# Three weight transfers at the seam change their order, and four sums move into the next step

## The chip, the cores and the metric

One core of a Trainium2 chip runs the whole kernel. The metric is the device time of one execution in microseconds. TensorE is called PE (its weight loads PEld), VectorE DVE, ScalarE ACT, GpSimd POOL; SP is the engine that issues most transfers.

## The reference

Two blocks follow one another. The first is a Mamba-2 scan over 4 batches, 8 heads, 768 positions in chunks of 32. The second routes 3072 tokens of 256 channels to one of 8 experts by a hash of the token's id:

```python
for c in range(nc):
    M = einsum('bhin,bhjn->bhij', Cc, Bc) * (exp(cum_i - cum_j) * causal)
    y[:, :, sl] = einsum('bhij,bhjd->bhid', M, xc) + einsum('bhin,bhnd->bhid', Cc, state) * exp(cum)
    state = decay_full * state + sum(Bx)
x = y.transpose(0, 2, 1, 3).reshape(3072, 256)
expert_idx = token_ids * 2654435761 % 8
for e in range(8):                     # w1[e]: 256 x 1024, w2[e]: 1024 x 256
    mask = expert_idx == e
    out[mask] = maximum(x[mask] @ w1[e], 0) @ w2[e]
```

## The kernel before, in words

The order on every engine is written out by hand; each engine and each DMA queue takes its instructions in that order, and waits by semaphores.

**First part.** The scan goes over 12 pieces of 64 positions in each sequence, two for each turn of a loop over `k`. Beside it the routing is worked out. Experts are sorted by their token count; what comes out first is *place* 0, the next place 1, and so on. The tokens of place `p` go into slots of a long row, in two halves (`p`, 0) and (`p`, 1) of `HALF[p]` tokens (202, 200, 198, 192, ...). The row is cut into tiles of 128 tokens. The first halves of places 0 to 3 lie in tiles 0 to 6, whose tokens are known early; tiles 7 and 8 hold the second half of place 0.

**Second part.** Each expert's two matrix products are done by a scheme with seven products instead of eight: `up(p, q0, what)` is one of the seven of the first layer for two of its four column blocks, `down(p, what)` one of the second layer's. Products 1 and 2 of `up` read only the first halves of the weights (`k` = 0, 1 of columns 0 to 511) and of the tokens. The others read sums: `sums_x` over tokens (DVE), `sums_w(p, layer, i, engine)` over weights (128 x 512 elements each, both operands in SBUF, four for a place and layer), `sums_h` over the hidden rows (DVE). Each `up` group is four matmuls into a PSUM bank of its own, and DVE or ACT drains the bank before the next product on it.

**The weights.** `load_w1(p, i)` asks for half `i` of place `p`'s first matrix (512 KB) on SP's queue; `load_w2(p)` for the second matrix (1 MB). (0, 0), (0, 1), (1, 0) and (2, 0) are asked for inside the first part. Place 3's buffer lies in memory that the first part gives back.

**The seam.** Between the parts stands the stretch from line 1025 to 1053. SP asks for (1, 1), (2, 1) and (3, 0), and POOL for the gathers of tiles 7, 8, 9 and 10. Then follow 16 groups (`m` = 0 to 15), products 1 and 2 of places 0 to 3, in the order of `seq`: the last four (`m` = 12 to 15) are place 3's and read (3, 0). DVE turns early tiles (`early`), and makes place 0's second two weight sums at `m` = 5, place 1's four at `m` = 8 and place 2's four at `m` = 11. At `m` = 13 and 14 PE turns tile 7 and tile 8, ahead of that `m`'s matmuls (`turn`: two transposes into bank 6, a copy by ACT); at `m` = 15 DVE makes the four sums over place 0's tokens. Behind the first group SP has a transfer of four bytes that waits for tile 8's gather (`held`), and behind that `load_w2(0)`, `load_w1(3, 1)` and `load_w2(1)`.

**The steps.** `step(p)` runs rounds `r`: in each a product of `up` for place `p`, both column blocks, and one of `down` for place `p - 1`. Step 0 has five rounds (products 6, 7, 5, 4, 3) and no `down`. POOL makes the weight sums of the second layer in it, `sums_w(0, 2, i)`, one in a round. DVE drains the banks, makes the sums over place 1's tokens from round 2 on, and begins step 1 with `sums_h(0, 0)`.

Of the kernel before, what the change touches and what calls it, by code (L numbers as in the profile page):

```python
# [25 lines left out]
def kernel(  # L26
# [12 lines left out]
    dve, act, pe, pool_e, sp_e = nc.vector, nc.scalar, nc.tensor, nc.gpsimd, nc.sync  # L39
# [7 lines left out]
    E, _, F = moe_w1.shape  # L47
# [564 lines left out]
    def load_w1(p, i, eng=sp_e):  # L612
        if p not in w1s:
            w1s[p] = (w4[0] if p % 4 == 3 else wpool).tile([P, DP, F], F32, name="w1")
        src = moe_w1[bass.ds(regs[p], 1), :, i * FH:(i + 1) * FH].rearrange("e (k p) f -> p (e k) f", p=P)
        eng.dma_start(out=w1s[p][:, :, i * FH:(i + 1) * FH], in_=src)

    def load_w2(p, eng=sp_e):
        w2s[p] = wx[0].tile([P, FP, DM], F32, name="w2", bufs=2)
        eng.dma_start(out=w2s[p], in_=moe_w2[bass.ds(regs[p], 1)].rearrange("e (k p) d -> p (e k) d", p=P))  # L620
# [139 lines left out]
    def early(m):  # L760
        turn_pair([q for q in EK if q // 2 == m], (3, 2, 7, 6)[m], dve)
# [3 lines left out]
    def sums_w(p, layer, i, eng):  # L765

        if layer == 1:
            w = w1s[p]
            q = lambda i, k: w[:, k, i * FH:(i + 1) * FH]
            if p not in s1:  # L770
                s1[p] = (spool if p % 3 else s1pool).tile([P, 4, FH], F32, name="s1")
            s = s1[p]
        else:
            w = w2s[p]
            q = lambda i, k: w[:, k * Q4:(k + 1) * Q4, i * P:(i + 1) * P]
            if p not in s2:
                s2[p] = spool.tile([P, 4, Q4, P], F32, name="s2")
            s = s2[p]
        i = (2, 1, 3, 0)[i]
        a_, b_, o = ((q(1, 0), q(1, 1), OP.add), (s[:, 2], q(1, 1), OP.add), (q(1, 0), q(0, 0), OP.subtract),  # L780
                     (q(0, 1), s[:, 1], OP.subtract))[i]
        eng.tensor_tensor(out=s[:, i], in0=a_, in1=b_, op=o)  # L782
        if eng is pool_e and i in (0, 3):
            eng.tensor_copy(out=space, in_=s[:, i, 0, 0:1] if layer == 2 else s[:, i, 0:1])
# [90 lines left out]
    def sums_x(p, i):  # L875
        n = HALF[p]
        q = lambda k, j: xT[:, k, slots(p, j)]
        if i == 0:
            t1[p] = mwork.tile([P, 4, N0], F32, name="t1")
        t = t1[p][:, :, 0:n]  # L880
        a_, b_ = ((q(0, 1), q(0, 0)), (q(1, 1), t[:, 0]), (q(0, 1), q(1, 1)), (q(1, 0), t[:, 1]))[i]
        dve.tensor_tensor(out=t[:, i], in0=a_, in1=b_, op=OP.subtract)  # L882

    def sums_h(p, i):
        n = HALF[p]
        if i == 0:
            t2[p] = hpool.tile([P, 4, Q4, N0], F32, name="t2", bufs=1)
        t = t2[p][:, :, :, 0:n]
        q = lambda k, j: hx[p][:, {(0, 1): 0, (1, 0): 1, (1, 1): 2}[k, j], :, 0:n]
        if i == 0:  # L890
            dve.scalar_tensor_tensor(out=t[:, 0], in0=q(0, 1), scalar=0.0, in1=h11[p][:, :, 0:n],
                                     op0=OP.max, op1=OP.subtract)
        elif i == 1:
            dve.tensor_tensor(out=t[:, 1], in0=q(1, 1), in1=t[:, 0], op=OP.subtract)
        elif i == 2:
            dve.scalar_tensor_tensor(out=t[:, 2], in0=q(0, 1), scalar=0.0, in1=q(1, 1), op0=OP.max, op1=OP.subtract)  # L896
        else:
            dve.tensor_tensor(out=t[:, 3], in0=q(1, 0), in1=t[:, 1], op=OP.subtract)
# [100 lines left out]
    def scatter(o_sb, idx):  # L999
        st = pool_e.indirect_dma_start(  # L1000
            out=out[:], out_offset=bass.IndirectOffsetOnAxis(ap=idx, axis=0),
            in_=o_sb, in_offset=None, bounds_check=NT - 1, oob_is_err=False)
        tc.declare_no_dep(st.ins, group="out_rows", reason="distinct rows")
        tc.add_to_no_dep_group("out_rows", st.ins)
# [12 lines left out]
    def turn(k):  # L1017
        if k not in turned:
            turn_x(k, XB)
            turned.add(k)  # L1020
# [1 line left out]
    need = lambda p: [k for k in tiles_of(p) if k not in EK] if p < E else []  # L1022
    outs = sorted(range(NK), key=lambda k: (done_at[k], k))

    for w in ((1, 1), (2, 1), (3, 0)):
        load_w1(*w)
    ask(need(0))
    first = [(p, q0) for p in range(NEAR) for q0 in (0, 2)]
# [3 lines left out]
    for m, (what, i) in enumerate(seq):  # L1032
        if m in (2, 6, 10):
            early((m + 2) // 4)
        if m == 5:
            for j in range(2, 4):
                sums_w(0, 1, j, dve)
        if m == 8:
            for j in range(4):
                sums_w(1, 1, j, dve)  # L1040
        if m == 11:
            for j in range(4):
                sums_w(2, 1, j, dve)
        if m in (13, 14):
            turn(need(0)[m - 13])
        if m == 15:
            for j in range(4):
                sums_x(0, j)
        up(*first[i], what, banks=(i % 6,) * 2)
        if m == 0:  # L1050
            sp_e.dma_start(out=held[:], in_=xg[need(0)[-1]][0:1, 0:1])
            for w in (0, (3, 1), 1):
                load_w2(w) if isinstance(w, int) else load_w1(*w)

    UP = [1, 6, 2, 7, 5, 4, 3]
    UP_E = [6, 7, 5, 4, 3]
    DOWN = [1, 2, 6, 5, 7, 4, 3]

    def step(p):

        ups = [] if p == E else UP_E if p < NEAR else UP
        downs = DOWN if p > 0 else []
        turns = [k for k in need(p + 1) if k not in turned]
        puts = [k for k in outs if done_at[k] == p - 2]
        gets = [k for w in ((2,), (3, 4))[p] for k in need(w) if k not in asked] if p < 2 else need(p + 3)
        sums = [(p, 2, i) for i in range(4)] if p < E else []
        sums += [(p + 2, 1, i) for i in range(4)] if 0 < p < E - 2 else []
        xs_ = [(p + 1, i) for i in range(4)] if p + 1 < E else []
        R = 5 if p == 0 else 7
        off = 0 if p == 0 else (R - len(ups)) // 2  # L1070
        sent = []
        for r in range(R):
            if p > 0 and (r == 0 or p >= NEAR and r < 4):
                sums_h(p - 1, r)
            if sent:
                scatter(*sent.pop(0))
            if gets and p == 0:
                ask(gets)
                gets = []
            if 0 <= r - off < len(ups):  # L1080
                up(p, 0, ups[r - off])
            if turns:
                turn(turns.pop(0))
            if puts:
                sent.append(put(puts.pop(0)))
            if sums and not (p == 1 and r < 4):
                sums_w(*sums.pop(0), pool_e)
            if gets and r >= 1:
                ask([gets.pop(0)])
            if 0 <= r - off < len(ups):  # L1090
                up(p, 2, ups[r - off])
            if 0 < p < NEAR and 0 < r < 4:
                sums_h(p - 1, r)
            if sums and r == 3 and p != 1:
                sums_w(*sums.pop(0), pool_e)
            if p >= NEAR and r >= 3 and not turns and xs_:
                sums_x(*xs_.pop(0))
            if p == 1 and r == 4:
                pool_e.tensor_copy(out=space, in_=t2[0][:, 3, 0, 0:1])
            if p == E - 1 and r == R - 1:  # L1100
                sums_h(p, 0)
            if downs:
                down(p - 1, downs[r])
                if downs[r] == 4 and p + 1 < E:
                    load_w2(p + 1)
            if p < NEAR and r >= (2 if p == 0 else 3) and not turns and xs_:
                sums_x(*xs_.pop(0))
        while xs_ or turns:
            if turns:
                turn(turns.pop(0))  # L1110
            else:
                sums_x(*xs_.pop(0))
        for o in sent:
            scatter(*o)
        for v in sums:
            sums_w(*v, pool_e)
        if p + 4 < E:
            load_w1(p + 4, 0)
            load_w1(p + 4, 1)
        for k in gets:  # L1120
            ask([k])

    for p in range(E):
        step(p)
# [48 lines left out]
    for m in range(2):  # L1173
        scatter(o_own[m], idx_out[:, rest[m]:rest[m] + 1])

    _, rn = nc.values_load_multi_w_load_instructions(
        nov_i[0:1, 0:1], min_val=0, max_val=NCH + E,
        skip_runtime_bounds_check_because="a count of tiles: at most one an expert besides the full ones")
    kf = route.tile([P, 1], F32)
    dve.memset(kf, float(NK))  # L1180
    with tc.For_i(0, rn[0], 1):
# [9 lines left out]
        for c in range(NCH):  # L1191
# [14 lines left out]
        _, re = nc.values_load_multi_w_load_instructions(  # L1206
            ei_i[0:1, 0:1], engines=[ET.SP], min_val=0, max_val=E - 1,
            skip_runtime_bounds_check_because="an expert's number, clamped to E - 1")
# [52 lines left out]
```

## Time and profile before

| | us |
|---|---|
| three runs | 231.1, 235.72, 237.67 |
| their median | 235.72 |
| the profiled execution | 231.41 |
| its span | 229.7 |
| PE busy | 213.5 |
| DVE busy | 180.7 |
| POOL busy | 172.4 |

The profile is that of one execution; its times count from the start of the span. The granted clock of PE was full up to the end of the work.

### The profile page before, as it was taken

The numbers are of one execution on the slowest core, as the hardware profiler recorded it, in microseconds if no ns is written. First come the engines' busy times: TensorE is split into PE (matmuls) and PEld (weight loads), VectorE is DVE, ScalarE is ACT, GpSimd is POOL, SyncE is SP. The second block draws the span as 40 slices with busy tenths as digits, with TensorE's granted clock in tenths as the row PEclk, the third lists the DMA queues.
The fourth block names the chain that finished last, engine by engine and source line by source line (L and its number), as shares of the span: only waits on it lengthen the run. The fifth ranks groups of instructions, "written<-read, shape, count | busy, mean of one in ns | idle before, by whom it ended". The sixth has DMA issues, their size and how long they took to land.

```text
span 229.7 us, 5853 instructions
## 1 busy us (share of the span) xinstructions
PE 213.5 (93%) x2266; PEld 200.5 (87%) x2266; DVE 180.7 (79%) x314; ACT 89.4 (39%) x190; POOL 172.4 (75%) x220
## 2 busy tenths in 40 slices
PE   6889989998786899999999999999999999999990
PEld 2778878877685799999999999999999999999980
DVE  7868899798547688899997998697489979956630
ACT  4774965954443551312123214234323411413210
POOL 7977367866717198489988998999799999996342
PEclk9999999999999999999999999999999999999996
DMA  6999799999888885029019119307005112401011
GB/s 136 162 200 127 181 191 177 174 185 302 273 218 259 253 267 199 24 75 332 30 62 334 64 47 339 118 7 244 26 24 204 33 45 79 175 23 47 24 70 43
DMA packets 49877, 33.16 MB, mean 144 GB/s; under 512 B 26632, under 2 KB 44184, under 8 KB 49850
## 3 DMA queue, kind: packets, MB, share of 16 engines
q1 hardware_dynamic: 46786, 25.76, 45.6%
q0 software_dynamic: 2400, 6.43, 8.5%
q10 hardware_dynamic: 664, 0.61, 1.1%
q8 instruction: 18, 0.29, 0.5%
q14 instruction: 9, 0.07, 0.1%
HBM read 26.49 MB, written 6.42 MB: 143 GB/s over the span
## 4 chain that ended last, share of the span: by engine, by line
PE 73%; DMA 8%; DVE 7%; ACT 6%; issue 2%; SPq 1%; POOL 1%; ACTq 0%; DVEq 0%; POOLq 0%
PE ps L964 31%; PE ps L917 28%; PE ps L315 4%; DMA w<-in_moe_w_dram 3%; DMA xg<-y_tokens,idx_in 3%; PE ps L991 2%; PE ps L374 2%; PE ps L636 2%; DMA y_tokens<-y_sb 2%; DVE m L321 1%; ACT z L358 1%; PE ps L387 1%; PE ps L269 1%; DVE rows L259 1%; ACT ct L289 1%
## 5 line engine op out<-in xcount | busy, mean ns | idle before, releaser
L628 POOL DMA_INDIRECT xg<-y_tokens,idx_in x25 | 30.2, 1206 | 17.1 <-issue 10.1
L917 PE MATMUL ps<-t,s 128*128 128x202 f32 (+7 forms) x192 | 37.1, 328 | 0.6 <-DVE t L882 0.6
L782 POOL TENSOR_TENSOR s<-w 128x512 f32<-128x512 f32 x26 | 33.2, 1277 | 5.7 <-DMA w<-in_moe_w_dram 5.5
L1000 POOL DMA_INDIRECT out_dram<-o_sb,idx_out x25 | 26.4, 1056 | 12.5 <-ACT o_sb L996 6.7
L964 PE MATMUL ps<-t,s 128*128 128x202 f32 (+7 forms) x192 | 35.5, 326 | 0.0
L917 PEld LDWEIGHTS ps<-t,s 128*128 128x128 f32 x192 | 31.5, 190 | 1.3 <-ACT h L927 0.9
L964 PEld LDWEIGHTS ps<-t,s 128*128 128x128 f32 x192 | 31.8, 189 | 0.3 <-issue 0.3
L917 PE MATMUL ps<-xT,w 128*128 128x200 f32 (+7 forms) x128 | 24.9, 329 | 3.0 <-DMA w<-in_moe_w_dram 2.3
L917 PEld LDWEIGHTS ps<-xT,w 128*128 128x128 f32 x128 | 20.7, 190 | 3.8 <-DVE s L782 2.5
L945 ACT ACTIVATE hx<-hx 128x404 f32<-128x404 f32 (+7 forms) x16 | 8.3, 525 | 31.8 <-DVE hx L944 31.3
L321 DVE COPY_PREDICATED m<-cmask,ps 128x1024 f32<-128x1024 int32 x12 | 15.5, 1320 | 3.6 <-PE ps L315 3.6
L782 POOL TENSOR_TENSOR s<-w,s 128x512 f32<-128x512 f32 x13 | 17.6, 1351 | 0.5
L782 POOL TENSOR_TENSOR s<-s,w 128x512 f32<-128x512 f32 x13 | 17.3, 1327 | 0.5
L882 DVE TENSOR_TENSOR t<-xT 128x202 f32<-128x202 f32 (+7 forms) x16 | 16.4, 1024 | 0.8 <-ACT xT L642 0.8
L923 ACT ACTIVATE p<-ps 128x404 f32<-128x404 f32 (+7 forms) x16 | 7.9, 492 | 20.0 <-PE ps L917 19.7
L374 PEld LDWEIGHTS ps<-x_t,m 128*64 128x64 f32 x384 | 12.1, 138 | 3.0 <-issue 1.3
L374 PE MATMUL ps<-x_t,m 128*64 128x64 f32 x384 | 13.4, 224 | 1.1 <-ACT y_sb L401 0.6
L315 PE MATMUL ps<-ce,bt 32*64 32x128 f32 x384 | 12.9, 274 | 1.1 <-ACT ce L289 0.7
L882 DVE TENSOR_TENSOR t<-xT,t 128x202 f32<-128x202 f32 (+7 forms) x16 | 13.7, 854 | 0.0
L896 DVE SCALAR_TENSOR_TENSOR t<-hx 128x808 f32<-128x808 f32 (+7 forms) x8 | 13.3, 1660 | 0.0
L315 PEld LDWEIGHTS ps<-ce,bt 32*64 32x64 f32 x384 | 10.4, 132 | 2.5 <-ACT ce L289 0.9
L358 ACT ACTIVATE z<-z,half 128x256 f32<-128x256 f32 x22 | 10.0, 504 | 6.6 <-DVE z L352 6.6
(201 smaller groups left out, 472.5 us busy)
## 6 DMA issues: line engine op xcount, KB each, us to landing
w<-in_moe_w_dram SPq DMA_DIRECT2D x16, 512.0 KB, 7.1
w<-in_moe_w_dram SPq DMA_DIRECT2D x8, 1024.0 KB, 8.0
x_t<-in_x_dram SPq DMA_DIRECT2D x12, 256.0 KB, 6.2
y_tokens<-y_sb SPq DMA_DIRECT2D x10, 256.0 KB, 4.3
raw<-in_B_dram SPq DMA_DIRECT2D x12, 128.0 KB, 3.5
raw<-in_C_dram SPq DMA_DIRECT2D x12, 128.0 KB, 3.5
y_tokens<-y_sb ACTq DMA_DIRECT2D x2, 256.0 KB
xg<-y_tokens,idx_in POOLq DMA_INDIRECT x25, 3.5
```

The source lines that it names most:

```text
L315: pe.matmul(out=ps[u * T:(u + 1) * T, GB + g, b * P:(b + 1) * P].rearrange("q (e i) -> q e i", e=2), lhsT=bts[ck][r, b, c], rhs=ces[ck][r, ...
L321: dve.copy_predicated(out=m_sb[k % 2][:, g0:g1].rearrange("q g b i -> q g (b i)"), mask=cmask.bitcast(I32).rearrange("q j i -> q (j i)").u ...
L358: act.activation(z4s[un][:, :, j], zs[un].rearrange("q b e d -> q b (e d)"), AF.Copy, scale=half4[:, j:j + 1])
L374: pe.matmul(out=o, lhsT=m_sb[k % 2][:, g, b, e * T:(e + 1) * T], rhs=xs[k][:, b, 2 * g + e], start=first(g // 2 * 2 + b % 2, c), stop=True ...
L628: pool_e.indirect_dma_start(out=xg[k], out_offset=None, in_=y_dram[0:n, :], in_offset=bass.IndirectOffsetOnAxis(ap=idx_in[:, k:k + 1], axi ...
L782: eng.tensor_tensor(out=s[:, i], in0=a_, in1=b_, op=o)
L882: dve.tensor_tensor(out=t[:, i], in0=a_, in1=b_, op=OP.subtract)
L896: dve.scalar_tensor_tensor(out=t[:, 2], in0=q(0, 1), scalar=0.0, in1=q(1, 1), op0=OP.max, op1=OP.subtract)
L917: pe.matmul(out=ps[:, bank, i * n:(i + 1) * n], lhsT=lhs[:, (q0 + i) * P:(q0 + i + 1) * P], rhs=rhs, start=(first and i == 0), stop=True, ...
L945: act.activation(hq(2), hq(2), AF.Relu)
L964: pe.matmul(out=ps[:, bank, 0:n], lhsT=lhs(q), rhs=rhs(q), start=(first and q == 0), stop=True, skip_group_check=True)
L1000: st = pool_e.indirect_dma_start(out=out[:], out_offset=bass.IndirectOffsetOnAxis(ap=idx, axis=0), in_=o_sb, in_offset=None, bounds_check= ...
```

## The change

The three transfers of the seam are asked for as (1, 1), (3, 0), (2, 1). The four sums of place 2's first layer leave the seam, and DVE makes one of them behind each of the first four rounds' `up` groups in step 0.

```diff
-    for w in ((1, 1), (2, 1), (3, 0)):
+    for w in ((1, 1), (3, 0), (2, 1)):
         load_w1(*w)
...
-        if m == 11:
-            for j in range(4):
-                sums_w(2, 1, j, dve)
...
+    late_sums = [0, 1, 2, 3]
...
             if p == E - 1 and r == R - 1:
                 sums_h(p, 0)
+            if p == 0:
+                for _ in range((1, 1, 1, 1, 0)[r]):
+                    sums_w(2, 1, late_sums.pop(0), dve)
             if downs:
                 down(p - 1, downs[r])
```

## Rows read from the trace of the kernel before

**Rows 1.** The page, busy time of each engine (share of the span) and instructions.

```profile
PE 213.5 (93%) x2266; PEld 200.5 (87%) x2266; DVE 180.7 (79%) x314; ACT 89.4 (39%) x190; POOL 172.4 (75%) x220
```

**Rows 2.** Waits of PE, 56 to 125 us: who for whom, total, times, longest.

```profile
PE ps L917 <- DMA w<-in_moe_w_dram: 2.3, 1, 2.3
```

**Rows 3.** Chain that ended last, in order of time: start, us, what.

```profile
66.55 7.14 DMA w<-in_moe_w_dram
...
76.53 0.38 DVE t L882
```

**Rows 4.** Timeline of the seam: start, us, engine, line, operation, count, idle before.

```profile
69.97 0.69 DVE L782 TENSOR_TENSOR s<-w 128x512 f32<-128x512 f32 x1 [1.98 <-DMA w<-in_moe_w_dram]
70.02 1.53 PE L917 MATMUL ps<-xT,w 128*128 128x198 f32 x8
...
72.97 0.68 DVE L782 TENSOR_TENSOR s<-w 128x512 f32<-128x512 f32 x1
...
73.82 0.89 PE L917 MATMUL ps<-xT,w 128*128 128x192 f32 x4 [2.27 <-DMA w<-in_moe_w_dram]
...
74.43 0.32 SPq L1051 DMA_DIRECT2D held<-xg  x1
74.55 0.38 PE L636 MATMUL ps<-ident,xg 128*128 128x128 f32 x2
...
75.13 0.38 ACT L642 ACTIVATE xT<-ps 128x256 f32<-128x256 f32 x1
...
75.57 0.44 PE L636 MATMUL ps<-ident,xg 128*128 128x128 f32 x2
...
77.34 0.49 ACT L927 ACTIVATE h<-ps 128x384 f32<-128x384 f32 x1 [0.16 <-PE ps L917]
...
77.89 0.95 PE L917 MATMUL ps<-t,s 128*128 128x202 f32 x4 [0.58 <-DVE t L882]
```

**Rows 5.** POOL's timeline, then gathers issued from 68 to 69 us: count, us to landing.

```profile
68.26 1.00 POOL L628 DMA_INDIRECT xg<-y_tokens,idx_in  x1 [5.31 <-DMA y_tokens<-y_sb]
...
xg<-y_tokens,idx_in POOLq DMA_INDIRECT x1, 5.8
```

**Rows 6.** Timeline of step 0 and the start of step 1.

```profile
80.71 1.27 POOL L782 TENSOR_TENSOR s<-w 128x512 f32<-128x512 f32 x1 [5.46 <-DMA w<-in_moe_w_dram]
...
83.33 0.36 DVE L882 TENSOR_TENSOR t<-xT 128x200 f32<-128x200 f32 x1
...
84.70 0.36 DVE L882 TENSOR_TENSOR t<-xT,t 128x200 f32<-128x200 f32 x1
...
86.07 0.51 DVE L882 TENSOR_TENSOR t<-xT 128x200 f32<-128x200 f32 x1
...
86.77 0.99 DVE L891 SCALAR_TENSOR_TENSOR t<-hx,h 128x808 f32<-128x808 f32 x1
...
86.96 1.51 PE L917 MATMUL ps<-t,s 128*128 128x200 f32 x8
...
87.84 1.25 DVE L932 TENSOR_TENSOR u<-ps,p 128x400 f32<-128x400 f32 x2
...
89.01 1.00 DVE L894 TENSOR_TENSOR t<-hx,t 128x808 f32<-128x808 f32 x1
...
89.69 1.52 PE L917 MATMUL ps<-t,s 128*128 128x200 f32 x8
...
91.04 1.53 PE L964 MATMUL ps<-t,s 128*128 128x202 f32 x8
```

**Rows 7.** Busy time in a stretch: length, then PE, PEld, DVE, ACT, POOL.

```profile
78.95:86.77 7.82, 7.82 (x48) 7.61 (x48) 6.77 (x14) 3.31 (x7) 5.62 (x6) 1.00 0.88 281
```

**Rows 8.** Timeline of step 1's end and step 2's start.

```profile
101.07 1.90 DVE L882 TENSOR_TENSOR t<-xT 128x198 f32<-128x198 f32 x1
...
101.46 1.28 POOL L782 TENSOR_TENSOR s<-w 128x512 f32<-128x512 f32 x1
...
103.75 0.83 PE L917 MATMUL ps<-t,s 128*128 128x198 f32 x4
```

## The prediction

> **What bounds the kernel now.** I read the page first: TensorE (PE) is busy for 213.5 of 229.7 us [rows 1], so time is saved only where PE stands still, and lost where it is made to. Second, who PE waited for between 56 and 125 us: the longest wait, 2.3 us once, is for a weight transfer [rows 2]. Third, the chain of work that ended last, in order of time: a weight transfer issued at 66.55 and landing 7.14 later, at 73.69, is a link of it [rows 3]. The reader is to see that this is place 3's first half, (3,0), the last of the three transfers that the seam asks for, and that PE went idle at 70.02 + 1.53 = 71.55 and began that place's matmuls at 73.82 [rows 4]. So the order of the three transfers is on the path.
>
> Fourth, what else arrives just then. The seam's last matmul groups stand behind two turned tiles, 7 and 8. Tile 7's gather was issued at 68.26 and landed 5.8 later, at 74.06 [rows 5]. Tile 8's landing is seen on SP: the small transfer that waits for it alone started at 74.43 [rows 4]. Both come after (3,0). So PE's 2.3 us can't all be won: two more arrivals lie 0.4 and 0.7 us behind the one that is moved.
>
> Fifth, VectorE (DVE) in step 0. Between its first drain there, at 78.95, and the start of the first sum over the hidden rows, at 86.77, it was busy for 6.77 of 7.82 us [rows 6, 7]. It has 1.05 us free there, and the change puts four operations in.
>
> **The change, part by part.** *(3,0) goes second.* The transfer that is second now landed by 72.97, since DVE's sums from it started then without waiting for a transfer [rows 4]; the first landed before 69.97. Equal transfers in the same place should land alike, so (3,0) lands between 71.8 (halfway from 69.97 to 73.69) and 72.97; I take 72.4, an estimate. PE starts the first group 0.13 after the landing now (73.69 to 73.82), so at 72.5; its four matmuls are done by 73.4. Then it meets tile 7: landed 74.06, with the same 0.13 the turn starts at 74.2 instead of 74.55. ScalarE's (ACT's) copy of it started 0.58 after the turn and took 0.38, so it ends at 74.2 + 0.58 + 0.38 = 75.16 instead of 75.51. The turn of tile 8 uses the same bank, waits for that copy, and started 0.06 after it: 75.2 instead of 75.57. From there on the chain is the one of before: two groups, ACT's last drain (77.34, 0.49 long), step 0's first matmul at 77.89 [rows 4]. The whole seam moves by 75.57 - 75.2 = 0.37 us. The bounds are 0 (the gathers share the transfer engines, and may be pushed back by as much) and 1.3 (the whole way from 73.69 to 72.4, if the gathers land earlier too).
>
> *(2,1) goes third.* It lands at about 73.7, and its first reader is now a DVE sum at about 79.8: no cost, with 6 us of cover. On SP nothing but these two issues change places; the transfers behind them wait for tile 8 as before, until 74.43.
>
> *Four sums leave the seam.* They ran on DVE from 72.97 to about 75.7 (4 x 0.69 on). DVE's next work, the sums over tile 8, waited for ACT's copy and started at 76.53 [rows 3, 4], 0.8 us after they were done. So their going frees nothing on the path.
>
> *Four sums come to step 0.* Each takes 0.69 us, as the first of their kind at 69.97 did [rows 4]: 4 x 0.69 = 2.76 us on DVE, one behind each of the first four rounds' second matmul group. Behind each on the DVE queue stand the drains of the next round and the sums for step 1, and PE waits for those through its banks. Of 2.76 us, 1.05 fill DVE's idle time [rows 7]; 1.71 remain as lag by the time the hidden sums begin. How much lag can PE bear? Three places [rows 6]: the first group of step 1 at 86.96 wants the sum that ran from 84.70 to 85.06 (margin 1.9); the next group at 89.69 writes to the bank that DVE's drain of 87.84, first of two and 0.58 long, empties (1.27); the second-layer group at 91.04 wants the sum of 89.01, 1.00 long (1.03). The last is the tightest: 1.71 - 1.03 = 0.68 us of PE stall.
>
> *The price of company.* In that same stretch GpSimd (POOL) makes its four sums, 1.27 us each, nearly without a gap from 80.71, when its weights land [rows 6]. They can't move forward: these weights are asked for behind tile 8. DVE's operations with both operands in SBUF sometimes wait for such a POOL sum. The sum of 101.07 took 1.90 us against 0.36 for one of the same kind at 83.33, and ended at 102.97, just behind POOL's sum of 101.46 to 102.74 [rows 6, 8]. Near to our place the wait is small: 0.36, 0.36 and 0.51 for the sums of 83.33, 84.70 and 86.07, beside POOL's sums [rows 6], so 0, 0 and 0.15. The first new sum starts before POOL does; three lie in POOL's stretch. By the nearest rows they cost 0 to 0.15 each, 0 to 0.45 together; by the far row 1.54 each (1.90 - 0.36), 4.6 together. The nearest rows are in the very stretch, so I take their upper half, 0.3. No gain is possible here, since a wait can't be negative; a new sum that holds POOL up only delays sums that PE reads a step later.
>
> *Who reads the late sums.* Step 2's first such group started at 103.75 [rows 8], 16 us or more behind them. No cost.
>
> The sum: -0.37 + 0.68 + 0.3 = +0.6 us. The profiled execution took 231.41 us, 1.7 more than its span of 229.7; it becomes 232.0 with +0.6. The three runs of before are 231.1, 235.72 and 237.67, so the profiled one is near the fastest, and the median is 4.3 above it. I carry +0.6 to the median: 235.72 + 0.6 = 236.3.
>
> **The rivals.** *A, POOL wins each time, slower.* If each of the three sums in POOL's stretch is issued just after POOL has begun one of its own, and waits it out as the sum of 101.07 did, the lag is 1.71 + 4.6 = 6.3, the stall 6.3 - 1.03 = 5.3, and the change 5.3 - 0.37 = +4.9 us: 236.3 by the profile, 240.6 by the median, 2.1%. It decides from the point at which a sum on DVE takes over 2 us. For it: POOL has hardly a gap from 80.71 to 86.4. Against it: the three sums of step 1 beside the same POOL work lost 0.15 in all, for DVE got in as POOL changed from one sum to the next. The Trainium skill, page SBUF — State Buffer, section Who interferes with whom, speaks for this rival: a VectorE instruction with two SBUF inputs contends with a GpSimd instruction that reads SBUF, and the one issued second blocks fully until the first is done. By that rule all that counts is the order of issue; the row of 101.07 agrees (1.90 us), those of 83.33 and 84.70 show issues that met no lock.
>
> *B, the seam gives all, faster.* The gathers land behind the weights now; if (3,0)'s earlier end lets them in earlier, the seam gives 1.3 us, and if the late sums fall into DVE's idle time and the margin, nothing is lost: -1.3, so 230.1 by the profile and 234.4 by the median. For it: 1.05 + 1.03 us of slack against 2.76. Against it: that leaves 0.68 over, and the bytes ahead of the gathers are the same.
>
> *C, the order doesn't help.* (3,0) goes into memory that the kernel's first part has to give back. If its issue waits for that, or if tile 7 lands later by what (3,0) gained, the seam gives 0 and the sums still cost 0.98: +1.0, 232.4 and 236.7. For it: PE stood waiting for the gathers too, by the landings above. Against it: the issue at 66.55 followed the one ahead of it directly.
>
> **How the numbers follow.** Forecast (by its bounds +0.3 to +0.8) 0.65; C 0.15; B 0.12; A 0.08. All but A stay within 2% (4.7 us), which is about what a measurement of this kernel can tell from no change. The executions differ by 6.6 us among themselves, far more than the forecast and B and C do, so the range is that of the runs with the cases laid on: from 231.1, the fastest, by B and the forecast mixed at about +0.2, 231.3; up to 237.67 + 1.0 = 238.7 by C. A's 240.6 and the rest of B stay outside. Chances: slower by over 2% A's 0.08 and 0.02 for the runs' scatter; faster by over 2% only by scatter, 0.07; no difference 0.83.
>
> **What would show it.** In the profile of the changed kernel PE's wait for the weight transfer at the seam should shrink from 2.3 to about 1, and a second wait of about 1, for tile 7's gather, should take its place; step 0's first matmul should start about 0.4 us earlier, near 77.5. The four sums should appear on DVE between 79 and 86, each 0.7 to 0.9 long. PE should wait for DVE between 86 and 92, near 1 us in all, where it had no wait, and the matmuls at about 101.8 should come 0.6 later than before. The prediction is wrong if the gathers land earlier than 74.0 (B), if PE starts step 0 no earlier than 77.8 (C), if PE's stall behind the late sums is under 0.3 or over 2 us, or if something outside the stretch from 66 to 102 us changes by more than that.

## The result, and the profile after

Over 22 runs of each kernel the median went from 235.1 us (231.1 to 238.69) to 236.12 us (233.04 to 239.42); the ratio is 1.0105, 95% interval [1.0062, 1.0149]. A ratio is taken over those runs of each kernel that lie within 1.5% of its own fastest, so the medians of all runs stand beside it here. Two later timings of the changed kernel gave 1.001 [0.997, 1.0051], medians 239.22 against 240.37 before, and 1.0058 [0.9989, 1.0127], medians 235.46 against 235.75. So the change makes a difference of less than 2%: the first timing has the changed kernel slower by 0.6 to 1.5%, the two later ones can't tell it from the kernel before. The forecast was +0.6 us on the median, +1.0 was measured in the first timing.

Executions already differ ahead of the seam, where nothing was changed: tile 7's gather was asked for at 68.26 us before and at 71.76 in the profiled execution of the changed kernel. So stretches are compared here, and not spans.

The page of the changed kernel, with the granted clock in 40 slices:

```profile
span 235.2 us, 5852 instructions
...
PE 218.0 (93%) x2266; PEld 203.5 (87%) x2266; DVE 180.8 (77%) x314; ACT 89.1 (38%) x190; POOL 173.1 (74%) x220
...
PEclk9799999999998999999999999999999999999998
```

Its timeline from the seam to step 1:

```profile
78.28 0.32 SPq L1048 DMA_DIRECT2D held<-xg  x1
...
79.33 0.38 PE L636 MATMUL ps<-ident,xg 128*128 128x128 f32 x2
...
82.67 0.95 PE L917 MATMUL ps<-t,s 128*128 128x202 f32 x4 [0.58 <-DVE t L882]
...
84.33 1.28 POOL L782 TENSOR_TENSOR s<-w 128x512 f32<-128x512 f32 x1 [6.12 <-ACT xT L642]
...
85.06 1.10 DVE L782 TENSOR_TENSOR s<-w 128x512 f32<-128x512 f32 x1
...
85.69 1.60 POOL L782 TENSOR_TENSOR s<-s,w 128x512 f32<-128x512 f32 x1
...
87.05 0.79 DVE L782 TENSOR_TENSOR s<-s,w 128x512 f32<-128x512 f32 x1
...
88.74 0.79 DVE L782 TENSOR_TENSOR s<-w,s 128x512 f32<-128x512 f32 x1
...
90.70 0.79 DVE L782 TENSOR_TENSOR s<-w 128x512 f32<-128x512 f32 x1
...
94.20 1.28 POOL L782 TENSOR_TENSOR s<-w 128x512 f32<-128x512 f32 x1
94.74 1.62 PE L917 MATMUL ps<-t,s 128*128 128x200 f32 x8
...
95.09 1.26 DVE L894 TENSOR_TENSOR t<-hx,t 128x808 f32<-128x808 f32 x1
...
96.50 1.61 PE L964 MATMUL ps<-t,s 128*128 128x202 f32 x8
...
102.03 1.53 PE L964 MATMUL ps<-t,s 128*128 128x202 f32 x8
```

The group that answers to the last line, in the kernel before:

```profile
96.49 1.53 PE L964 MATMUL ps<-t,s 128*128 128x202 f32 x8
```

The reader is to see two things. The four late sums are there and take 1.10, 0.79, 0.79 and 0.79 instead of 0.69, while POOL's sum of 85.69 takes 1.60 instead of 1.27: they wait for one another. The second sum over the hidden rows, at 95.09 beside POOL's sum of 94.20, takes 1.26 instead of 1.00. And the two PE groups that want DVE's drain and DVE's hidden sum [rows 6] begin 12.07 and 13.83 us after step 0's first matmul (94.74 and 96.50 less 82.67), where they began 11.80 and 13.15 after it (89.69 and 91.04 less 77.89). The last group shown, which drains into the work tile `du3`, began 18.60 after it before (96.49 less 77.89) and begins 19.36 after it now (102.03 less 82.67). From there to the end nothing differs: 133.2 us in both (229.7 less 96.49, 235.2 less 102.03). I call the way from step 0's first matmul to that group *the stretch*; in the changed kernel it holds all that the late sums cost.

This trace says little on the seam. PE was behind when tile 8 landed (78.28): it turned tile 7 only at 79.33, after it had run from 70 to 75 us at a mean granted clock of 0.71.

### The profile page after: what moved, and what is told of

It reads as the page before. It is cut to its first block, busy times and chain, and to the rows that moved or that the text cites. A ratio compares the mean times of both kernels' runs of the same rounds, so it can differ in the third digit from the quotient of the medians.

```text
span 235.2 us, 5852 instructions
## 1 busy us (share of the span) xinstructions
PE 218.0 (93%) x2266; PEld 203.5 (87%) x2266; DVE 180.8 (77%) x314; ACT 89.1 (38%) x190; POOL 173.1 (74%) x220
## 4 chain that ended last, share of the span: by engine, by line
PE 69%; DMA 9%; DVE 8%; ACT 7%; issue 4%; POOL 1%; SPq 1%; DVEq 0%; POOLq 0%; ACTq 0%
PE ps L964 30%; PE ps L917 23%; PE ps L315 4%; DMA xg<-y_tokens,idx_in 4%; PE ps L374 2%; DMA w<-in_moe_w_dram 2%; PE ps L991 2%; DMA y_tokens<-y_sb 2%; DVE m L321 1%; PE ps L269 1%; ACT z L358 1%; PE ps L636 1%; PE ps L387 1%; ACT ce L289 1%; DVE s L782 1%
## 5 line engine op out<-in xcount | busy, mean ns | idle before, releaser
L628 POOL DMA_INDIRECT xg<-y_tokens,idx_in x25 | 29.5, 1180 | 19.8 <-issue 7.0
L917 PE MATMUL ps<-xT,w 128*128 128x200 f32 (+7 forms) x128 | 26.4, 344 | 0.8 <-DVE xT L654 0.8
L917 PEld LDWEIGHTS ps<-xT,w 128*128 128x128 f32 x128 | 22.4, 202 | 1.3 <-DVE xT L654 1.2
L945 ACT ACTIVATE hx<-hx 128x404 f32<-128x404 f32 (+7 forms) x16 | 8.3, 525 | 33.0 <-DVE hx L944 32.6
L942 ACT ACTIVATE hx<-hx 128x404 f32<-128x404 f32 (+7 forms) x16 | 8.2, 525 | 11.3 <-DVE hx L941 10.9
```

The source lines that it names most:

```text
L628: pool_e.indirect_dma_start(out=xg[k], out_offset=None, in_=y_dram[0:n, :], in_offset=bass.IndirectOffsetOnAxis(ap=idx_in[:, k:k + 1], axi ...
L917: pe.matmul(out=ps[:, bank, i * n:(i + 1) * n], lhsT=lhs[:, (q0 + i) * P:(q0 + i + 1) * P], rhs=rhs, start=(first and i == 0), stop=True, ...
L942: act.activation(hq(1), hq(1), AF.Relu)
L945: act.activation(hq(2), hq(2), AF.Relu)
```

## The experiments

The table has four times of each traced execution. The first two count from the issue of tile 7's gather: to the start of the transfer that waits for tile 8's gather (tile 8 has landed), and to step 0's first matmul. The third is the difference of the two, with what else held PE in brackets. The fourth is the stretch. "Late" is the number of place 2's sums in step 0.

| run | late | tile 7's issue to tile 8 | tile 7's issue to step 0 | tile 8 to step 0 | stretch |
|---|---|---|---|---|---|
| before | 0 | 6.17 | 9.63 | 3.46 | 18.60 |
| changed kernel, first trace | 4 | 6.52 | 10.91 | 4.39 (PE behind) | 19.36 |
| e0, changed kernel again | 4 | 7.83 | 10.89 | 3.06 | 20.59 |
| e11, a third time | 4 | 7.45 | 12.04 | 4.59 (clock) | 19.40 |
| e1, order only | 0 | 7.58 | 10.73 | 3.15 | 18.57 |
| e10, order only again | 0 | 7.41 | 10.76 | 3.35 | 18.57 |
| e4, order, copy first | 0 | 7.41 | 10.56 | 3.15 | 18.57 |
| e2, sums only | 4 | 7.19 | 11.02 | 3.83 (weights) | 20.16 |
| e3, (2,1) behind the gathers | 0 | 5.84 | 11.09 | 5.25 (copy) | 18.60 |
| e7, the same, copy first | 0 | 5.47 | 10.37 | 4.90 (PE behind) | 18.60 |
| e5, POOL quiet for place 0 | 4 | 7.19 | 11.65 | 4.46 (clock) | 19.51 |
| e8, POOL quiet for 0 and 1 | 4 | 7.64 | 10.75 | 3.11 | 18.60 |
| e6, two and two | 2 | 7.77 | 10.50 | 2.73 | 18.61 |
| e9, two and two again | 2 | 6.02 | 10.77 | 4.75 (PE behind) | 19.67 |

**e0, the changed kernel again** (no edit).

> The changed kernel again, for a second trace of it: in the first one the early tiles' gathers came some 4 us late and TensorE's clock fell ahead of the seam, so that its seam doesn't show what the new order does. Theory (T): the seam gives little, because tile 7's and tile 8's gathers bind behind the weights; step 0 and step 1 lose 0.7 to 1.0 us to the late sums. From step 0's first matmul to the second-layer group that drains into du3 (18.60 us before, 19.36 in the first trace after) about 19.4; from the issue of tile 7's gather to step 0's first matmul 9.2 to 9.4 (9.63 before). Rival (R1): the late sums cost nothing in step 0 and the loss comes from the seam: 18.6 and over 10. In all +0.3 to +1.5 us against the kernel before.

The stretch was 20.59, so the late sums cost 2.0 us here, more than T's 0.7 to 1.0. From tile 7's issue to step 0 it took 10.89 and not T's 9.2 to 9.4; that is over R1's 10, but R1's stretch of 18.6 is not what came. The timeline:

```profile
79.39 0.92 PE L917 MATMUL ps<-xT,w 128*128 128x192 f32 x4 [1.84 <-DVE s L782]
...
80.81 0.44 PE L636 MATMUL ps<-ident,xg 128*128 128x128 f32 x2 [0.51 <-DMA xg<-y_tokens,idx_in]
...
80.99 0.32 SPq L1048 DMA_DIRECT2D held<-xg  x1
...
84.05 0.95 PE L917 MATMUL ps<-t,s 128*128 128x202 f32 x4 [0.58 <-ACT h L927]
...
90.46 1.60 POOL L782 TENSOR_TENSOR s<-w,s 128x512 f32<-128x512 f32 x1
...
90.86 1.43 DVE L882 TENSOR_TENSOR t<-xT 128x200 f32<-128x200 f32 x1
...
94.45 1.62 PE L917 MATMUL ps<-t,s 128*128 128x200 f32 x8 [1.16 <-DVE t L882]
```

Besides the late sums, a sum over tokens lost its turn: the one of 90.86 took 1.43 instead of 0.36, since POOL's sum of 90.46 ran until 92.06, and PE then waited 1.16. On the seam the trace shows the wait that I had missed: place 3's first group is held 1.84 us not by its weights but by DVE, whose copy of tile 6 stands behind place 1's four sums. After it PE waits 0.51 for tile 7's gather, as forecast.

**e1, the order alone.**

```diff
-    for w in ((1, 1), (2, 1), (3, 0)):
+    for w in ((1, 1), (3, 0), (2, 1)):
```

> Only the order of the three transfers is changed; place 2's four sums stay in the seam, where VectorE waits for tile 8 anyway. T: step 0's stretch is 18.6 as before, and the seam is 0.2 to 0.4 us shorter than before (9.2 to 9.4 from tile 7's gather to step 0), since the sums end at about 76.4 and the sums over tile 8's tokens begin there: -0.3 us in all, the best of the two halves. Rival (R1): the order is what costs; the seam is longer than 9.63, and the kernel slower than before by the whole 1 us or more.

0.992 [0.9871, 0.997], medians 238.02 against 240.37. Its timeline on the seam:

```profile
73.22 1.00 POOL L628 DMA_INDIRECT xg<-y_tokens,idx_in  x1 [6.16 <-DMA y_tokens<-y_sb]
...
80.37 0.69 DVE L782 TENSOR_TENSOR s<-w 128x512 f32<-128x512 f32 x1 [0.85 <-DMA w<-in_moe_w_dram]
...
80.80 0.32 SPq L1051 DMA_DIRECT2D held<-xg  x1
...
83.95 0.92 PE L917 MATMUL ps<-t,s 128*128 128x202 f32 x4 [0.67 <-DVE t L882]
```

The stretch is 18.57, as T says. The seam is not: from tile 7's issue to step 0 it took 10.73, over R1's 9.63, where T had 9.2 to 9.4. R1's slower kernel did not come either; the time fell, and by more than T gives.

**e2, the sums alone.** The changed kernel with the three transfers in the order of before.

> Only the four sums are moved to step 0; the transfers keep the order of before. T: the seam is that of before (9.6), TensorE waits 2 us for place 3's first half there when the early tiles come in time, and step 0's stretch is 19.4: +0.8 us in all. Rival (R1): step 0's stretch stays 18.6, and the kernel is as fast as before.

1.004 [0.9988, 1.0091], medians 241.13 against 240.37; the stretch is 20.16, 1.56 longer, where T had 0.8. R1 falls. Its timeline:

```profile
71.61 1.00 POOL L628 DMA_INDIRECT xg<-y_tokens,idx_in  x1 [6.14 <-DMA y_tokens<-y_sb]
...
78.56 0.89 PE L917 MATMUL ps<-xT,w 128*128 128x192 f32 x4 [1.22 <-DMA w<-in_moe_w_dram]
78.80 0.32 SPq L1048 DMA_DIRECT2D held<-xg  x1
...
82.63 0.95 PE L917 MATMUL ps<-t,s 128*128 128x202 f32 x4 [0.58 <-DVE t L882]
...
89.00 1.43 DVE L882 TENSOR_TENSOR t<-xT 128x200 f32<-128x200 f32 x1
```

Again one sum over tokens waited out a POOL sum (1.43). On the seam PE waited 1.22 for the weights, and step 0 came 11.02 after tile 7's issue, where T had 9.6.

This run is also the trace of the old order on the chip of e0 and e1. In all three tile 7's gather was asked for 2.83 us behind the first of the three weight transfers (issued at 68.78 here, 70.33 in e0, 70.39 in e1). With the old order tile 8 had landed 7.19 us after tile 7's issue, with the new one 7.83 and 7.58, later by 0.4 to 0.6. Step 0 began 11.02, 10.89 and 10.73 after that issue, earlier by 0.1 to 0.3. So in these traces a good part of what (3,0) gained went back to the gathers, as rival C has it. It is one trace of the old order, so the size isn't firm.

**e3, the third transfer behind the gathers.**

```diff
-    for w in ((1, 1), (3, 0), (2, 1)):
+    for w in ((1, 1), (3, 0)):
...
-            for w in (0, (3, 1), 1):
+            for w in (0, (2, 1), (3, 1), 1):
...
-            if p == 0:
-                for _ in range((1, 1, 1, 1, 0)[r]):
+            if p == 1:
+                for _ in range((0, 0, 1, 1, 1, 1, 0)[r]):
```

> Place 2's second half, (2,1), is asked for only behind tile 8's gather, after the second-layer weights of place 0, and its four sums are made in rounds 2 to 5 of step 1. Only 1 MB of weights is then ahead of the two gathers. T (gathers bind behind the weights): tile 7 and tile 8 land 0.8 to 1.5 us sooner after their issue (5.8 and 4.9 before), the seam from tile 7's gather to step 0 is 8.0 to 8.8 instead of 9.63; the sums cost up to 0.7 in step 1: -0.3 to -1.3 in all. Rival (R2): the gathers' time is their own and not the weights': the landings and the seam stay as before, and the sums' cost in step 1 leaves +0.3 to +0.8.

0.9934 [0.9881, 0.9987], medians 239.39 against 240.37. Its timeline on the seam:

```profile
73.19 1.00 POOL L628 DMA_INDIRECT xg<-y_tokens,idx_in  x1 [7.57 <-DMA y_tokens<-y_sb]
...
79.03 0.32 SPq L1048 DMA_DIRECT2D held<-xg  x1
79.11 0.69 DVE L782 TENSOR_TENSOR s<-w 128x512 f32<-128x512 f32 x1
...
79.71 0.42 DVE L654 COPY xT<-ps 128x256 f32<-128x256 f32 x1
...
80.18 0.92 PE L917 MATMUL ps<-xT,w 128*128 128x192 f32 x4 [2.65 <-DVE xT L654]
...
84.28 0.95 PE L917 MATMUL ps<-t,s 128*128 128x202 f32 x4 [0.58 <-DVE t L882]
```

With 1 MB of weights ahead of them instead of 1.5, the gathers were in 5.84 us after tile 7's issue (73.19 to 79.03); in e0, e1 and e2, on the same chip and asked for as long behind the weights, it took 7.83, 7.58 and 7.19. So the gathers do share with the weights, as T says. (How long behind matters too: before and in e9, 3.44 and 4.79 us behind the first weights, they took 6.17 and 6.02 with all 1.5 MB ahead.) But step 0 gained nothing from it, and came 11.09 after tile 7's issue, not 8.0 to 8.8: the copy of tile 6, at 79.71, became the last arrival (2.65 us of wait). The four sums, now in step 1, lie behind the stretch, and cost 0.8 us there: from its end to the end of the span it took 134.0 us (236.9 less 102.88) instead of 133.2.

**e4, order alone, the copy first.** e1 with place 1's sums moved behind the copy of tile 6.

```diff
-        if m == 8:
+        if m == 11:
             for j in range(4):
                 sums_w(1, 1, j, dve)
```

> The order of the transfers changed, the four sums left in the seam, and VectorE's copy of the early tile 6 put ahead of place 1's four sums, which it stood behind. Theory (T2): with the new order place 3's first group waits no longer for its weights but for that copy (2.3 us in the trace with the order alone), and ahead of the sums the wait goes; but tiles 7 and 8 land when they did, and the eight sums on VectorE end when they did, so step 0 begins no more than 0.2 us sooner after tile 8's landing than with the order alone (3.15 us): same time as that, 0.5 to 1% under the kernel before. Rival (R3): the copy is the bound of the seam, and step 0 begins 1 us or more sooner after tile 7's issue (under 9.7 where it was 10.73).

1.0018 [0.9961, 1.0076], medians 238.28 against 239.72; step 0 at 3.15 behind tile 8, as in e1, and 10.56 behind tile 7's issue. R3 falls: with the weights in the order of e1 the copy is not what step 0 waits for; the gathers are (PE waited 1.20 us for tile 7's).

**e7, e3 with the copy first**, its sums in rounds 1 to 4 of step 1.

> (2,1) asked for behind tile 8's gather, its sums in rounds 1 to 4 of step 1, and the copy of tile 6 ahead of place 1's sums. T2: the gathers land 5.8 to 6.2 us after tile 7's issue as they did with (2,1) behind them, and now TensorE isn't held by the copy (2.65 us there), so the seam from tile 7's gather to step 0 is 8.7 to 9.5 instead of 11.09; the sums cost up to 0.7 in step 1 and 2. In all 0.7 to 1.5% under the kernel before, the fastest of all. Rival (R3): another wait takes the copy's place, the seam stays over 10, and the kernel is as fast as with the copy behind (0.993).

0.994 [0.9886, 0.9994], medians 238.6 against 239.72; tile 7's issue to step 0 took 10.37 us, not 8.7 to 9.5, which is R3's side. The gathers were in after 5.47, and there was no wait for the copy of tile 6, but PE was itself behind, having run at a granted clock of 0.66 from 70 to 75 us. This run can't say what the seam would give at full clock. Behind the stretch its sums cost 1.2 us (237.5 less 103.09 is 134.4).

**e5 and e8, GpSimd quiet.** The changed kernel, with POOL's second-layer sums of place 0 (e5), or of places 0 and 1 (e8), replaced by zeros written without a read, so that these sums are left out of the result. The edit of e8:

```diff
-        eng.tensor_tensor(out=s[:, i], in0=a_, in1=b_, op=o)
+        if layer == 2 and p in (0, 1):
+            eng.memset(s[:, i], 0.0)
+        else:
+            eng.tensor_tensor(out=s[:, i], in0=a_, in1=b_, op=o)
```

> The changed kernel, but GpSimd fills the four second-layer sums of place 0 with zeros instead of reading weights for them, so those sums are left out of the result. T (port): the late sums then meet no GpSimd operation that reads SBUF, and the stretch from step 0's first matmul to the group that drains into du3 falls to 18.6 to 19.2 (19.35 and 20.60 in the two traces of the changed kernel, 18.60 before), each late sum takes 0.69. Rival (R4): the loss is only the 2.76 us of VectorE's work against its slack, and the stretch stays at 19.3 or more.

> The changed kernel with GpSimd filling the second-layer sums of places 0 and 1 with zeros, so that those eight sums are left out of the result and GpSimd reads no weights from step 0 to the middle of step 1. In the run with place 0's alone left out, a sum of place 1 came forward into step 0's place and one of VectorE's sums over tokens waited 1.07 us for it. T (port): with that gone too, every SBUF operation on VectorE there keeps its own duration (late sums 0.68, sums over tokens 0.36), and the stretch from step 0's first matmul to du3's group is 18.6 to 19.0: what is left of the 0.68 us that was worked out without any wait for GpSimd. Rival (R4): VectorE's load alone makes the loss, and the stretch is 19.3 or more.

In e5 the late sums took 0.68 each, but the stretch was 19.51, over T's 19.2 and on R4's side. The company had only changed: with its sums gone, POOL came to a sum of place 1 sooner, at 96.28, and a sum over tokens issued at 96.53 took 1.43. The timeline of e8, one execution, where this one is gone too:

```profile
81.73 0.95 PE L920 MATMUL ps<-t,s 128*128 128x202 f32 x4 [0.58 <-DVE t L885]
...
84.12 0.68 DVE L785 TENSOR_TENSOR s<-w 128x512 f32<-128x512 f32 x1
...
85.81 0.68 DVE L785 TENSOR_TENSOR s<-s,w 128x512 f32<-128x512 f32 x1
...
87.39 0.68 DVE L785 TENSOR_TENSOR s<-w,s 128x512 f32<-128x512 f32 x1
...
89.23 0.68 DVE L785 TENSOR_TENSOR s<-w 128x512 f32<-128x512 f32 x1
...
91.64 0.98 DVE L894 SCALAR_TENSOR_TENSOR t<-hx,h 128x808 f32<-128x808 f32 x1
...
92.55 1.04 DVE L935 TENSOR_TENSOR u<-ps,p 128x400 f32<-128x400 f32 x2
...
93.51 0.98 DVE L897 TENSOR_TENSOR t<-hx,t 128x808 f32<-128x808 f32 x1
...
99.43 0.18 POOL L1100 COPY space<-t 128x1 f32<-128x1 f32 x1 [14.76 <-DVE t L901]
...
100.33 1.53 PE L967 MATMUL ps<-t,s 128*128 128x202 f32 x8
```

All four late sums are still there, 0.68 us each, and the stretch is 100.33 - 81.73 = 18.60, to the hundredth that of before. So the whole loss of the late sums is the meeting with POOL; DVE's load by itself costs nothing. R4 falls. What the run shows is a POOL that does nothing: with no weights to wait for, it wrote place 0's zeros ahead of the late sums, and later stood idle for 14.76 us, up to 99.43. Whether writes alone, beside a late sum, would cost anything is not shown.

**e6 and e9, two and two.** Copy first, two of place 2's sums in the seam and two in step 0.

```diff
+            for j in range(2):
+                sums_w(2, 1, j, dve)
...
-    late_sums = [0, 1, 2, 3]
+    late_sums = [2, 3]
...
-                for _ in range((1, 1, 1, 1, 0)[r]):
+                for _ in range((1, 1, 0, 0, 0)[r]):
```

> As with the copy first, and only two of place 2's sums move to step 0 (rounds 0 and 1); two stay in the seam. T (slack): 2 x 0.69 = 1.38 us is 0.33 over VectorE's free 1.05 and far under the margin of 1.03 behind that, so the stretch from step 0's first matmul to du3's group is 18.6 to 18.8; step 0 begins 2.8 to 3.1 us after tile 8's landing. In all 0.5 to 1% under the kernel before, as fast as the order alone or up to 0.5 us faster. Rival (R4): each late sum costs its share, half of 0.75 to 2.0 us, and the stretch is 19.0 to 19.6.

> Two sums in the seam, two in step 0, the copy of tile 6 first: the version that beat the kernel before by 0.3 to 2.2%, from 6 of its runs, timed again for a narrower interval. T: step 0's stretch 18.6 again, and 0.5 to 1% under the kernel before. Rival: that interval was luck of few runs, the version is within 0.3% of the kernel before.

The first timing, with 6 runs, gave 0.9878 [0.9783, 0.9973], medians 238.24 against 239.72, and a stretch of 18.61; the second, with 12, gave 1.0043 [0.9985, 1.0101], medians 234.74 against 235.62, and 19.67. In e6 one of the two late sums met POOL as well (1.12 us at 88.13), and the slack took it up. The trace of e9 shows how the same code comes to a loss:

```profile
84.75 1.27 POOL L782 TENSOR_TENSOR s<-w 128x512 f32<-128x512 f32 x1 [6.71 <-DMA w<-in_moe_w_dram]
...
84.96 1.60 DVE L782 TENSOR_TENSOR s<-w,s 128x512 f32<-128x512 f32 x1
...
94.44 2.17 DVE L894 TENSOR_TENSOR t<-hx,t 128x808 f32<-128x808 f32 x1
94.46 1.27 POOL L782 TENSOR_TENSOR s<-w 128x512 f32<-128x512 f32 x1
...
96.75 1.61 PE L964 MATMUL ps<-t,s 128*128 128x202 f32 x8 [0.66 <-DVE t L894]
```

POOL's weights landed 0.2 us ahead of the first late sum instead of behind it, so that sum took 1.60; DVE then came late enough to the hidden sum of 94.44 to meet POOL's next one there (2.17 instead of 1.00). Two late sums are not safe either; the slack argument for them falls.

**e10 and e11, order alone and changed kernel on one chip.**

> The order of the transfers alone, again, beside the changed kernel on one chip: the first timing gave 0.3 to 1.3% under the kernel before, but the version with the copy first, which differs from it only there, gave no difference. T: the seam gives 0.3 to 0.4 us behind tile 8's landing, nothing else changes: stretch of step 0 18.6, step 0 begins about 3.1 us after tile 8's landing, -0.3 us in all, which the timing can hardly tell from nothing. Rival (R5): the order alone gives 1 us or more, as the first timing said: 0.992 again.

> The changed kernel a third time, beside the order alone. T: its stretch of step 0 is longer than 18.6 by what the meetings with GpSimd cost in that execution, 0.7 to 2.1 us (0.75 and 2.00 so far), so it is 0.7 to 2.1 us slower than the order alone on the same chip, and 0.3 to 1.7 us slower than the kernel before. Rival (R4'): the meetings are rare, the stretch is 18.6 to 18.8 in this trace, and both versions take the same time.

The order alone: 0.9934 [0.9887, 0.9981], stretch 18.57, step 0 at 3.35 behind tile 8. The changed kernel: 1.0058 [0.9989, 1.0127], stretch 19.40. T is right that the stretch is longer, by 0.83. On what the order gives the ratio sides with R5, but the medians of all runs are 235.6 for the order alone, 235.46 for the changed kernel and 235.75 for the kernel before. So this timing doesn't settle which is the fastest.

## Why the prediction was right, and which steps of it failed

**The sum came out, its terms did not.** +0.6 was forecast and +1.0 measured on the median, inside the range. That is luck in good part. The term for DVE's lag (0.68) was 0, and the term for POOL's company (0.3) was 0.76, 0.80 and 1.99 us in the changed kernel's three traces and 1.56 in e2's (stretch less 18.60), 1.3 on average; the two errors nearly cancel. The signs that the prediction gave as points in time (74.0, 77.5, 77.8, 101.8) can't be read, since the executions differ by several us ahead of the seam. What the late sums cost PE stayed within its 0.3 to 2 us, in e0 at the edge.

**The seam, -0.37.** From tile 8's landing to step 0, 3.46 us became 3.06 in e0, the one trace of the changed kernel in which PE was neither behind nor slowed: -0.40. But this measure leaves out when tile 8 lands. From tile 7's issue, e0 and e1 gained only 0.1 to 0.3 on e2. The step that failed is that the landings of tiles 7 and 8 (74.06 and 74.43) stay where they were: tile 8 landed 0.4 to 0.6 later with the new order, which the prediction had as its lower bound and as rival C. That two arrivals stand close behind (3,0) was right. A second step failed, "PE starts the first group 0.13 after the landing": it starts after the copy of tile 6, which I had left out, since before the weights came later still. It cost nothing in e0, for tile 7 lands later yet.

**DVE's lag, 1.71.** This is the step that failed outright. In e8 the lag can be read without company: the hidden sums begin 9.91 us after step 0 (91.64 less 81.73), 8.88 before (86.77 less 77.89). The lag is 1.03, not 1.71. At the second hidden sum, where the margin of 1.03 counts, it is 0.66 (93.51 less 81.73 against 89.01 less 77.89), so no stall is left over. I had set 2.76 us of work against the idle time alone. From its first drain to the hidden sums DVE was busy for 8.57 of 8.85 us in e8, for 6.77 of 7.82 before [rows 7]: the four sums added 1.80 us of busy time, and 0.77 of it fell into idle time. A part of the difference is in the drains. Where DVE follows PE its two drains of a round take 1.25 [rows 6], and 1.04 to 1.05 once it is late and both wait for it (92.55 in e8). That slack lies inside the busy time, and no busy share shows it.

**The company, 0 to 0.45 by the near rows, 4.6 by the far one.** The near rows misled. Three token sums beside POOL's lost 0.15 because they are short and happened to be issued as POOL changed over. Now five or six operations with two SBUF operands stand in POOL's stretch, and in e0, e2 and e9 one of them each was issued just behind the start of a POOL sum and waited it out: 1.43, 1.43 and 1.60 where 0.36, 0.36 and 0.69 is their own time. That is rival A's mechanism, once in a step and not three times; in the first trace of the changed kernel there is no such wait, but four partial ones (1.10, 0.79, 0.79 and 0.79 instead of 0.69), and the hidden sum's (1.26 instead of 1.00, and 1.25 to 1.26 in e0, e2 and e11 too). Hence 0.8 to 2.0 us instead of its 5.3. The Trainium skill, page SBUF — State Buffer, section Who interferes with whom, calls the port pair that the two engines share an exclusive lock, and says that issue order decides who blocks; these three rows agree, each issued 0.2 to 0.4 us behind POOL's sum. By the same rule POOL's sums wait for DVE's, and they took 1.60 where one of DVE's was ahead (85.69 in the changed kernel).

Two other rows don't fit so well. The sum of 101.07, which the prediction counted for that rule [rows 8], is recorded as starting 0.39 us ahead of POOL's sum of 101.46, and the hidden sum of 94.44 in e9 0.02 ahead of POOL's; both waited it out all the same. Why is open.

**What stays open.** Two timings of the order alone gave ratios 0.8 and 0.7% under 1 (some 1.6 to 1.9 us), though the medians of the second lie only 0.15 us apart, while e4, which differs only in where the copy stands, gave none. The traces account for less. In e1 and e10 the third transfer's landing is seen where DVE waits for it, at 80.37 and 77.84; had (3,0) been third, step 0 would have begun as long after that as it did before, some 4.1 us (73.82 to 77.89): 84.5 and 81.9 instead of 83.95 and 81.41, so 0.5 us is saved, an estimate; against e2's trace it is 0.1 to 0.3. The rest of the 1.6 wasn't found in any trace. Nor is the ratio a sign of the seam alone: e3's is 0.9934 too, though its traced seam gained nothing and its sums cost 0.8 us further on. No trace exists of the changed kernel's seam in an execution in which tile 7 was asked for as early as in that of before.

**The half worth keeping.** By the traces the order alone is the better half. From tile 7's issue to the end of the span it took 162.5 us in e1 and in e10 (235.7 less 73.22, 233.2 less 70.65), and 163.4, 164.7 and 164.6 in the changed kernel's three traces. The ratios say the same on the chip of e10 and e11 (0.9934 and 1.0058 against the same runs), the medians there don't. In the seam the four sums are not quite free with the new order, since (2,1) lands last: PE waited 0.67 and 1.04 us for the sums over tile 8's tokens, which stand behind them on DVE, instead of 0.58, and step 0 came 3.15 and 3.35 behind tile 8, 3.06 and 3.11 in e0 and e8.

## What to carry to other kernels

Before work with two SBUF operands moves to VectorE, lay its new place beside GpSimd's own timeline: it is not the free share of either engine that counts, but whether GpSimd has such an operation of its own under way just then, and the cost changes from one execution to the next. An engine that follows another has more slack than its idle time shows. When a transfer on the path is moved forward, list what else arrives in the microsecond behind it, the copies in another engine's queue too, and measure from a point ahead of them all, so that a landing pushed back is seen, before the gain is counted.

## What the runs showed of the hardware

TensorE's granted clock fell somewhere between 66 and 88 us in seven of the thirteen other traces, and not in that of before, where it read 1.00 in every row from 60 to 85 us. In e11 it fell in the seam itself. The stretches of 2 us there (length; PE, PEld, DVE, ACT and POOL busy; granted clock; DMA share; GB/s):

```profile
74.00:76.00 2.00, 0.36 (x2) 0.36 (x3) 1.59 (x3) 0.00 (x0) 1.70 (x2) 1.00 0.55 173
76.00:78.00 2.00, 1.77 (x9) 1.48 (x8) 0.00 (x0) 0.88 (x2) 0.12 (x1) 0.70 0.27 90
78.00:80.00 2.00, 2.00 (x9) 1.91 (x8) 0.29 (x1) 0.81 (x2) 0.00 (x0) 0.50 0.37 98
80.00:82.00 2.00, 1.42 (x8) 1.12 (x7) 1.01 (x4) 0.98 (x2) 0.00 (x0) 0.95 1.08 383
```

PE had stood still for 2.43 us, until 75.64, before it fell to the lower of its two levels, 1.2 GHz, and eight matmuls that take 1.47 us at the higher level (e0, at 82.00) took 2.07. In the kernel before PE stood still for 2.27 us and in e3 for 2.65, without a fall. A fall ahead of the seam cost some 1.7 us: sixteen matmuls took 4.64 us in the changed kernel's first trace (at 69.48) and 2.99 in e0 (at 69.84). That is as much as all that was studied here, and may be part of why executions of one kernel differ by 6 us.
